# A fused state-space and GELU kernel: decay rows spread by transfers in place of products with ones, and the second weight's pieces queued first

## The chip, the cores and the metric

One Trainium2 chip, one of its cores. The metric is the device time of one launch in microseconds, the median of several runs. One further execution is taken by the hardware profiler; the views below come from it.

## The reference

First a Mamba-2 style scan over 4 batches, 8 heads, 768 positions, head size 32 and state size 16, in chunks of 32, then a feed-forward block over the 3072 tokens.

```python
log_a = np.log(np.clip(a, 1e-06, 1.0))
for c in range(nc):                       # chunks
    cum = np.cumsum(la, axis=-1)
    L = np.exp(cum[:, :, :, None] - cum[:, :, None, :]) * causal
    M = np.einsum('bhin,bhjn->bhij', Cc, Bc) * L
    y_intra = np.einsum('bhij,bhjd->bhid', M, xc)
    y_inter = np.einsum('bhin,bhnd->bhid', Cc, state) * np.exp(cum)[..., None]
    y[:, :, sl] = y_intra + y_inter
    state = decay_full * state + (Bc, xc outer products, decayed to the chunk's end)
x = y.transpose(0, 2, 1, 3).reshape(3072, 256)
h = x @ w_in                              # 256 x 2048
g = h * (1.0 / (1.0 + np.exp(-1.702 * h)))
out = g @ w_out                           # 2048 x 256
```

The two weights are float64 in memory; the kernel turns their bits into float32 on the chip. The other inputs are float32.

## The kernel before, in words

**Tiling.** The 768 positions of a batch are 6 chunks of 128 (NC), and each chunk is two halves of 64 (H), within which the decay matrix L is made. Work goes by *pairs* of chunks, all 8 heads at once: 12 pairs, 3 to a batch. Pairs are numbered over the batches, so pairs 0, 1 and 2 are batch 0 and pairs 3 to 5 batch 1. PG = 2 pairs make a *group* of 512 tokens (TG), and there are 6 groups. Pair 2 (PG) and pair 3 are group 1; pair 2 is the third and last pair of batch 0, and its rows are that batch's last 256 positions.

**Stages of a pair.** `decay(p)` makes L: one VectorE scan over the pair's a, spread over 128 partitions (`ra[p]`), against `idents`, a tile that starts a new product at the diagonal; `ends` multiplies B by L's last column into Be. `clip_rows(b)` and `decay_rows(b)` make `since[b]`, the decay since the start of a half, from the batch's a spread over partitions (`raf[b]`): clip on VectorE, the first elements set apart by GpSimd, a scan on VectorE. `turn(p)` transposes B and C on TensorE, ScalarE copies them from PSUM, and `since_start` multiplies C by `since` on VectorE, reading the transposed C in PSUM. `score` is the product C by B, `gain` the product Be by x into two PSUM banks A, `keep_both` turns A into states, `weigh` multiplies L by the scores, and `finish` has the products of y: step 0 from states (inter), step 1 from L and x (intra).

**The feed-forward block** of group 0 is `hidden(0, f)` for 16 values of f, two matmuls of 512 columns each and a Silu, and `project_all(0, ...)`, again 16 values of f with two matmuls of 512 columns each. Later groups do it by a seven-product scheme (`first`, `product`), with sums of weights prepared by `mix_in` and `mix_w` on VectorE.

**Weights.** w_in and w_out are read in 10 pieces (0 to 5 of w_in, 6 to 9 of w_out, 1 MB each for 4 to 9). `fetch(i)` issues the two transfers of a piece into one of 4 buffers of bits; `rounded`, `fields`, `clamp` and `join` convert it, on VectorE but for `clamp` on ScalarE. `narrow(i)` is `rounded(i)`, `fields(i + 1)`, `join(i)`. A buffer is free when the `join` of the piece before in it has read it.

**The order** is written out by hand. While `hidden(0, f)` and `project_all(0)` run, two tables, `in_hidden[0]` and `in_project[0]`, say what is put behind or ahead of which f:

```python
    at(in_hidden[0], 5, store_a, lambda: fetch(7), lambda: fetch(8),
       lambda: load(PG + 1))
    at(in_hidden[0], 9, lambda: fan_all(PG))
```

Every engine executes its instructions in that order (`in_order`). Nearly all transfers are issued by SyncE (SP), so its queue has the same order, and an issue that waits holds back all behind it. Transfers wait on one of 8 semaphores in turn, so a transfer is issued only after the eighth before it has landed.

**How a is spread.** The decay needs each row of a on 64 or 128 partitions. For pairs 0 and 1 it comes from logarithms and matmuls. `rows_a` loads a into `az`, four copies of 32 rows (one row to a batch and head); `clip(az)` clips it, sets each half's first element apart in `starts` and zeroes it. `store_a` then writes the 32 rows to a scratch tensor in DRAM, and for pair 3 and later `spread(p)` reads it back, the same 2 KB to each of 64 partitions (256 runs of 2 KB for a pair). `spread_rows(b)` does the like for a batch's rows straight from a. For pair 2 it is done by products with ones: `pick_a` (ScalarE) masks the rows by head, `fan_all` issues 8 matmuls with `ones` (`fan`, L412), then those of the last rows of batch 0 (`fan_since`, L501 and L530) with `whose`, then four VectorE scans straight from PSUM (`decay_heads`). `since_fanned` scans the last rows into `since[0]`.

The tile of `raf` has one buffer for all batches (tag "af", bufs=1).

Of the kernel before, what the change touches and what calls it, by code (L numbers as in the profile page):

```python
# [8 lines left out]
FP32 = mybir.dt.float32  # L9
# [26 lines left out]
def kernel(  # L36
# [69 lines left out]
    az = ffn.tile([P, 4 * TG // 2], FP32, tag="mg", name="az", bufs=3)[:, :NC * P].rearrange(  # L106
# [138 lines left out]
    def spread(p, held=False):  # L245

        if p - 2 in ra:
            ra[p] = ra[p - 2]
        else:
            ra[p] = words(f"a{p}").bitcast(FP32)[:, :2 * NH * H].rearrange(  # L250
                "p (k e) -> p k e", k=2)
        if held:
            nc.vector.memset(ra[p][:, 0, :1], 0.0)
        b, c = divmod(2 * p, NC)
        for i, side in enumerate(SIDES):
            nc.sync.dma_start(
                out=ra[p][side],
                in_=scratch[c:c + 2, i, b * NH:(b + 1) * NH].rearrange("c h i -> c (h i)").unsqueeze(
                    0).to_broadcast([H, 2, NH * H]))
# [3 lines left out]
    def spread_rows(b):  # L263
        raf[b] = raw.tile([P, NC, P], FP32, tag="af", name=f"af{b}", bufs=1)
        nc.sync.dma_start(out=raf[b].rearrange("p c s -> p (c s)"),
                          in_=a[b].unsqueeze(1).to_broadcast([NH, N, S]))

    def rows_a(t, queues):

        e = t.shape[1] * P  # L270
        for r in range(R):
            queues[r % len(queues)].dma_start(
                out=t[32 * r:32 * r + 32].rearrange("p c s -> p (c s)"),
                in_=a.rearrange("b h s -> (b h) s")[:, :e])
# [74 lines left out]
    starts, fans, flat = {}, {}, {}  # L349

    def clip(t, name):

        nc.vector.tensor_scalar(out=t, in0=t, scalar1=1e-6, scalar2=1.0,
                                op0=ALU.max, op1=ALU.min)
        starts[name] = const.tile([P, t.shape[1], 2], FP32, name=f"starts{name}")
        first = t.rearrange(by_chunk, s=2)[:, :, :, 0]
        nc.vector.tensor_copy(starts[name], first)
        nc.vector.memset(first, 0.0)

    def pick_a(p):  # L360

        b, c = divmod(2 * p, NC)
        X = ffn.tile([P, 2, DM], FP32, tag="ob", name=f"X{p}")
        X = fans[p] = X.rearrange("p k (q i) -> p k q i", q=Q)
        for q in range(Q):
            nc.scalar.activation(X[:, :, q], az[:, c:c + 2], AF.Copy, scale=pick[:, b, q:q + 1])

# [9 lines left out]
    pick = picker("pick", NB, 1, NH)  # L377
    whose = const.tile([32 * PG, 1 + PG, NH, N], FP32, name="whose")
    nc.gpsimd.memset(whose, 1.0)
    for i, n, head in ((0, 1, PG), (1, 2, PG), (0, 0, 1)):  # L380
        t = whose[32 * i:32 * i + 32, n:n + 1]
        nc.gpsimd.affine_select(out=t, in_=t, pattern=[[-1, 1], [-head, NH], [0, N]],
                                compare_op=ALU.is_equal, fill=0.0, base=-max(n - 1, 0),
                                channel_multiplier=1)
# [23 lines left out]
    def fan(p, r, ab):  # L408

        rows = slice(32 * r, 32 * r + 32)  # L410
        for i, side in enumerate(SIDES):
            nc.tensor.matmul(out=ab[side].rearrange("p (k q i) -> p k q i", k=2, q=Q),  # L412
                             lhsT=ones[rows, side], rhs=fans[p][rows][:, :, :, side],
                             start=True, stop=True, tile_position=(32 * r, H * i),
                             skip_group_check=True)

    def fan_all(p):

        ab = area(f"ab{p}")[:, :, :2 * Q * H]
        for r in range(R):  # L420
            fan(p, r, ab[:, r])
        fan_since()
        for r in range(R):
            decay_heads(p, r, ab[:, r])
        for k in range(2):
            ends(p, k)

# [15 lines left out]

    def decay_heads(p, r, ab):

        if r == 0:
            L = ssd.tile([P, R, 2 * Q * H], FP32, tag="L", name=f"L{p}", bufs=3)
            flat[p] = L
            Ls[p] = L.rearrange("p r (k q i) -> p k r q i", k=2, q=Q)
        nc.vector.tensor_tensor_scan(  # L450
            out=flat[p][:, r], data0=ab,
            data1=idents.rearrange("p h i -> p (h i)")[:, :2 * Q * H],
            initial=0.0, op0=ALU.mult, op1=ALU.add)
# [24 lines left out]
    def clip_rows(b):  # L478
        t = raf[b]
        nc.vector.tensor_scalar(out=t, in0=t, scalar1=1e-6, scalar2=1.0,  # L480
                                op0=ALU.max, op1=ALU.min)
        first = ssd.tile([P, NC, P], FP32, tag="first", name=f"first{b}", bufs=1)
        nc.gpsimd.memset(first, 0.0)
        f, t0 = (v.rearrange(by_chunk, s=2)[:, :, :, 0] for v in (first, t))
        nc.gpsimd.tensor_copy(f, t0)
        nc.gpsimd.memset(t0, 0.0)
        firsts[b] = first

    def decay_rows(b):

        t, first = raf.pop(b), firsts.pop(b)
        since[b] = ssd.tile([P, NC, P], FP32, tag="since", name=f"since{b}")
        nc.vector.tensor_tensor_scan(
            out=since[b].rearrange("p c s -> p (c s)"), data0=t.rearrange("p c s -> p (c s)"),
            data1=first.rearrange("p c s -> p (c s)"),
            initial=0.0, op0=ALU.mult, op1=ALU.add)

    def fan_rows(t, c0, c1, o):

        o = o[:, :(c1 - c0) * P]  # L500
        nc.tensor.matmul(out=o, lhsT=whose[:32, 0].rearrange("p h n -> p (h n)"),  # L501
                         rhs=t[:32, c0:c1].rearrange("p c s -> p (c s)"), start=True,
                         stop=True, tile_position=(0, 0), skip_group_check=True)
        return o

    def since_first():
# [3 lines left out]
        for p in range(PG):  # L510
            at = slice(32 * p, 32 * p + 32)
            nc.tensor.matmul(out=rows[p],
                             lhsT=whose[at, 1 + p].rearrange("p h n -> p (h n)"),
                             rhs=cum[at].rearrange("p k s -> p (k s)"), start=True, stop=True,
                             tile_position=(32 * p, 0), skip_group_check=True)
# [9 lines left out]

    def fan_since():
        o = bank("rows4")
        t = fanned["rows"] = fan_rows(az, CG, NC, o)
        f = fanned["starts"] = o[:, 2 * P:2 * P + 2 * (NC - CG)]
        nc.tensor.matmul(out=f, lhsT=whose[:32, 0].rearrange("p h n -> p (h n)"),  # L530
                         rhs=starts[1][:32, CG:].rearrange("p c s -> p (c s)"), start=True, stop=True,
                         tile_position=(0, 0), skip_group_check=True)

    fanned = {}

    def since_fanned():

        t, f = fanned["rows"], fanned["starts"]
        first = ssd.tile([P, NC, P], FP32, tag="first", name="first0", bufs=1)[:, CG:]
        nc.gpsimd.memset(first, 0.0)  # L540
        nc.vector.tensor_copy(first.rearrange(by_chunk, s=2)[:, :, :, 0],
                              f.rearrange("p (c s) -> p c s", s=2))
        nc.vector.tensor_tensor_scan(
            out=since[0][:, CG:].rearrange("p c s -> p (c s)"), data0=t,
            data1=first.rearrange("p c s -> p (c s)"), initial=0.0, op0=ALU.mult, op1=ALU.add)
# [38 lines left out]
    def area(name):  # L584
        return psa.tile([P, R, 4 * P], FP32, tag="cb", name=name)
# [605 lines left out]
    rows_a(az, (nc.sync,))  # L1191
# [20 lines left out]
    load(PG)  # L1212
# [7 lines left out]
    def store_a():  # L1220
        clip(az, 1)
        for i, side in enumerate(SIDES):
            nc.sync.dma_start(out=scratch[:, i].rearrange("c r i -> r c i"), in_=az[:32, :, side])

    at(in_hidden[0], 5, store_a, lambda: fetch(7), lambda: fetch(8),
       lambda: load(PG + 1))
    at(in_hidden[0], 6, lambda: pick_a(PG))
    at(in_hidden[0], 9, lambda: fan_all(PG))
    at(in_hidden[0], 9, since_fanned)
    for i, k, c in ((2, 1, 1), (3, 2, 2), (4, 4, 4), (5, 6, 8), (6, 9, 12), (7, 12, 15)):  # L1230
        at(in_hidden[0], k, lambda i=i: narrow(i))
        at(in_hidden[0], c, lambda i=i: clamp(i + 1))
    at(in_hidden[0], 9, lambda: spread(PG + 1), lambda: spread_rows(1))
    n, p = 2 * PG, 3 * PG
    pairs = PG, PG + 1
    at(in_project[0], 0, lambda: turn(PG), lambda: rounded(8), lambda: fold_ident(1),
       lambda: fields(9), lambda: join(8))
    at(in_project[0], 1, lambda: clamp(9))
    at(in_project[0], 2, lambda: decay(PG + 1), lambda: clip_rows(1),
       lambda: decay_rows(1), lambda: turn(PG + 1))  # L1240
    at(in_project[0], 5, lambda: narrow(9))
    at(in_project[0], 9, lambda: score(pairs), lambda: gain(pairs), lambda: keep_both(pairs, True),
# [202 lines left out]
```

## Time and profile before

| | us |
|---|---|
| median of 3 runs | 351.66 |
| lowest and highest | 350.62, 352.45 |
| the profiled execution, whole run | 349.68 |
| its span, first to last instruction | 347.8 |
| TensorE (PE) busy | 342.0 (98%) |
| VectorE (DVE) busy | 253.5 (73%) |
| ScalarE (ACT) busy | 153.1 (44%) |
| GpSimd (POOL) busy | 12.9 (4%) |

How to read it: the whole run is the span and some 1.9 us around it. PE is the matmuls, PEld the weight loads, which overlap them. Busy shares are means over the span; the stage with the change lies in its first quarter, from 17.8 us (first hidden unit) to 80 us (last product of group 0's projection). Times of single instructions are us from the span's start. In the chain of waits, each matmul counts twice or nearly so, since a float32 matmul leaves two records.

### The profile page before, as it was taken

The numbers are of one execution on the slowest core, as the hardware profiler recorded it, in microseconds if no ns is written. First come the engines' busy times: TensorE is split into PE (matmuls) and PEld (weight loads), VectorE is DVE, ScalarE is ACT, GpSimd is POOL, SyncE is SP. The second block draws the span as 40 slices with busy tenths as digits, with TensorE's granted clock in tenths as the row PEclk, the third lists the DMA queues.
The fourth block names the chain that finished last, engine by engine and source line by source line (L and its number), as shares of the span: only waits on it lengthen the run. The fifth ranks groups of instructions, "written<-read, shape, count | busy, mean of one in ns | idle before, by whom it ended". The sixth has DMA issues, their size and how long they took to land.

```text
span 347.8 us, 8141 instructions
## 1 busy us (share of the span) xinstructions
PE 342.0 (98%) x3392; PEld 271.9 (78%) x3392; DVE 253.5 (73%) x479; ACT 153.1 (44%) x349; POOL 12.9 (4%) x41
## 2 busy tenths in 40 slices
PE   8899999999999999999999999999999999999996
PEld 6644444557788888888888888888888888899996
DVE  5899999998679998839995649787555654455463
ACT  5698573107354324744332543442444321554320
POOL 8300000000000100000000000000000000000000
PEclk9999999999999999999999999999999999999999
DMA  6699997435526100435613036300000300000301
GB/s 162 142 336 193 283 212 155 81 77 93 105 58 128 33 2 15 63 104 102 101 28 50 2 81 117 64 2 1 2 2 2 61 2 0 0 2 0 62 0 61
DMA packets 89980, 25.92 MB, mean 75 GB/s; under 512 B 73432, under 2 KB 87128, under 8 KB 89944
## 3 DMA queue, kind: packets, MB, share of 16 engines
q1 hardware_dynamic: 89112, 24.88, 33.3%
q10 hardware_dynamic: 832, 0.52, 0.5%
q8 instruction: 26, 0.43, 0.5%
q14 instruction: 10, 0.08, 0.1%
HBM read 22.15 MB, written 3.24 MB: 73 GB/s over the span
## 4 chain that ended last, share of the span: by engine, by line
PE 97%; ACT 1%; DVE 1%; issue 0%; DVEq 0%
PE acc L1050 28%; PE X L945 20%; PE Y L955 14%; PE h L889 10%; PE o L987 8%; PE acc L1057 7%; PE y L833 2%; PE y L821 2%; PE cb L682 2%; PE A L713 1%; PE busy L440 1%; PE ab L554 1%; PE ab L548 0%; DVE steps L735 0%; ACT steps L730 0%; ACT drop L522 0%
## 5 line engine op out<-in xcount | busy, mean ns | idle before, releaser
L950 ACT ACTIVATE ac<-X 128x256 f32<-128x256 f32 x76 | 29.1, 383 | 78.6 <-PE X L945 78.2
L1050 PE MATMUL acc<-mg,mw 128*128 128x256 f32 x192 | 54.5, 379 | 0.0
L922 ACT ACTIVATE gT<-gT 128x512 f32<-128x512 f32 (+1 forms) x76 | 39.3, 520 | 34.1 <-DVE gT L1077 33.4
L1077 DVE TENSOR_TENSOR gT<-Y,ac 128x512 f32<-128x512 f32 x38 | 26.2, 689 | 36.1 <-PE Y L955 30.5
L945 PE MATMUL X<-my,mi 128*128 128x256 f32 x152 | 45.2, 380 | 0.0
L1077 DVE TENSOR_TENSOR gT<-Y,b 128x256 f32<-128x256 f32 x38 | 15.8, 419 | 35.2 <-PE Y L955 35.2
L1050 PEld LDWEIGHTS acc<-mg,mw 128*128 128x128 f32 x192 | 36.5, 190 | 5.0
L1050 PE MATMUL acc<-gT,w_out 128*128 128x256 f32 x128 | 35.5, 379 | 0.0
L889 PE MATMUL h<-yT,w_in 128*128 128x512 f32 (+2 forms) x98 | 35.5, 518 | 0.0
L945 PEld LDWEIGHTS X<-my,mi 128*128 128x128 f32 x152 | 28.0, 190 | 4.1 <-ACT ac L950 0.4
L889 PEld LDWEIGHTS h<-yT,w_in 128*128 128x128 f32 x98 | 17.0, 190 | 16.5 <-issue 14.3
L987 PE MATMUL o<-gT,w_out 128*128 128x512 f32 x64 | 28.6, 597 | 0.0
L913 DVE TENSOR_TENSOR mg<-gT 128x512 f32<-128x512 f32 x40 | 27.2, 681 | 0.0
L1050 PEld LDWEIGHTS acc<-gT,w_out 128*128 128x128 f32 x128 | 24.2, 190 | 3.4 <-ACT yT L860 0.2
L950 ACT ACTIVATE b<-X 128x256 f32<-128x256 f32 x38 | 14.6, 384 | 20.0 <-PE X L945 19.6
L945 PE MATMUL X<-yT,w_in 128*128 128x256 f32 x76 | 23.2, 389 | 0.0
L945 PE MATMUL X<-my,w_in 128*128 128x256 f32 x76 | 22.7, 382 | 0.2 <-issue 0.2
L955 PE MATMUL Y<-yT,w_in 128*128 128x256 f32 x76 | 22.7, 381 | 0.0
L955 PE MATMUL Y<-my,mi 128*128 128x256 f32 x76 | 22.6, 379 | 0.0
L955 PE MATMUL Y<-yT,mi 128*128 128x256 f32 x76 | 22.5, 379 | 0.0
L987 PEld LDWEIGHTS o<-gT,w_out 128*128 128x128 f32 x64 | 11.8, 190 | 13.2 <-issue 12.7
L402 DVE TENSOR_TENSOR_SCAN L<-a,idents 128x1024 f32<-128x1024 f32 x9 | 20.5, 2277 | 0.4 <-DMA a<-scratch 0.4
(156 smaller groups left out, 544.2 us busy)
## 6 DMA issues: line engine op xcount, KB each, us to landing
a<-scratch SPq DMA_DIRECT2D x18, 256.0 KB, 5.3
bits<-in_moe_w_out_dram SPq DMA_DIRECT2D x8, 512.0 KB, 5.4
x<-in_x_dram SPq DMA_DIRECT2D x24, 128.0 KB, 3.0
out_dram<-ob SPq DMA_DIRECT2D x40, 64.0 KB, 1.9
bits<-in_moe_w_in_dram SPq DMA_DIRECT2D x8, 256.0 KB, 4.6
bits<-in_moe_w_in_dram SPq DMA_DIRECT2D x4, 512.0 KB, 9.3
b<-in_B_dram SPq DMA_DIRECT2D x20, 64.0 KB, 3.0
af<-in_a_dram SPq DMA_DIRECT2D x3, 384.0 KB
```

Source lines behind the costliest of these rows:

```text
L402: nc.vector.tensor_tensor_scan(out=L, data0=ra[p].rearrange("p k e -> p (k e)"), data1=idents.rearrange("p h i -> p (h i)"), initial=0.0, ...
L682: nc.tensor.matmul(out=s["cb"][side, r, k].rearrange("p (q i) -> p q i", q=Q), lhsT=BT[rows, k, side], rhs=CT[rows, k, :, side], start=Tru ...
L889: nc.tensor.matmul(out=h[:, cols], lhsT=w_in[:, f, k], rhs=yT[g][:, k, cols], start=(k == 0 and e == 0), stop=(k == NK - 1), skip_group_ch ...
L913: nc.vector.tensor_tensor(out=t[:, 0:2], in0=B[:, :, 1], in1=B[:, 0], op=ALU.subtract)
L922: nc.scalar.activation(o, i, AF.Silu, scale=GELU_SCALE)
L945: nc.tensor.matmul(out=s["X"], lhsT=lhsT, rhs=rhs, start=i == "1", stop=i == "4", skip_group_check=True)
L950: nc.scalar.activation(copy, s["X"], AF.Copy)
L955: nc.tensor.matmul(out=o, lhsT=lhsT, rhs=rhs, start=s.pop("new", False), stop=i != "5", skip_group_check=True)
L987: nc.tensor.matmul(out=o[c], lhsT=w_out[:, c, f], rhs=gT[g, f // 2][:, f % 2], start=(f == 0), stop=(f == NF - 1), skip_group_check=True)
L1050: nc.tensor.matmul(out=acc[g][0][i][:, cols], lhsT=w, rhs=h[:, cols], start=(j == 0 and k == 0 and (i, 0) in begins), stop=(j == NF // 2 - ...
L1057: nc.tensor.matmul(out=o[k] if type(o) is list else o[:, cols], lhsT=h[:, cols], rhs=w, start=(j == 0 and (i, k) in begins), stop=(j == NF ...
L1077: nc.vector.tensor_tensor(out=o, in0=v, in1=w, op=ALU.add)
```

## The change

Pair 2's a and the last 256 positions' rows of batch 0 are spread by transfers like those of the later pairs. `az` has 32 rows only, loaded by one transfer. `clip`, `pick_a`, `fan`, `fan_all`, `decay_heads`, `fan_rows`, `fan_since`, `since_fanned`, the mask `pick` and a third of `whose` go. `spread(PG)` uses a buffer of yT. `spread_rows(0)` reads the last two chunks alone.

The order changes with it. On SyncE, piece 7 of w_out is fetched after f=3, piece 8 after f=5 behind the stores to scratch, then B and C of pair 2 (piece 9 follows when piece 5 is joined), after f=9 the rows of batch 0, the a of pair 2, B and C of pair 3, the a of pair 3, then the x of both; the rows of batch 1 come after f=4 of the projection and wait until the scan of batch 0's rows has freed their buffer. Before, B, C and x of pair 2 went ahead of pieces 7 and 8, and those of pair 3 ahead of piece 9. In the projection `turn(PG)` goes from f=0 to f=3, pair 2's decay is behind it, pair 3's block goes from f=2 to f=5, `narrow(9)` from f=5 to f=6, and `score` and `gain` from f=9 to f=10.

```diff
-    az = ffn.tile([P, 4 * TG // 2], FP32, tag="mg", name="az", bufs=3)[:, :NC * P].rearrange(
+    az = ffn.tile([P, 4 * TG // 2], FP32, tag="mg", name="az", bufs=3)[:32, :NC * P].rearrange(
...
     def spread(p, held=False):
 
-        if p - 2 in ra:
+        if p == PG:
+            ra[p] = ffn.tile([P, NK, TG], FP32, tag="yT", name=f"a{p}").rearrange(
+                "p (k x) s -> p k (x s)", k=2)
+        elif p - 2 in ra and p - 2 > PG:
             ra[p] = ra[p - 2]
...
     def spread_rows(b):
-        raf[b] = raw.tile([P, NC, P], FP32, tag="af", name=f"af{b}", bufs=1)
+        c = 0 if b else CG
+        raf[b] = raw.tile([P, NC, P], FP32, tag="af", name=f"af{b}", bufs=1)[:, c:]
         nc.sync.dma_start(out=raf[b].rearrange("p c s -> p (c s)"),
-                          in_=a[b].unsqueeze(1).to_broadcast([NH, N, S]))
+                          in_=a[b, :, c * P:].unsqueeze(1).to_broadcast([NH, N, S - c * P]))
...
-    rows_a(az, (nc.sync,))
+    nc.sync.dma_start(out=az.rearrange("p c s -> p (c s)"), in_=a.rearrange("b h s -> (b h) s"))
...
-    load(PG)
...
     def store_a():
-        clip(az, 1)
+        nc.vector.tensor_scalar(out=az, in0=az, scalar1=1e-6, scalar2=1.0, op0=ALU.max, op1=ALU.min)
+        nc.vector.memset(az.rearrange(by_chunk, s=2)[:, :, :, 0], 0.0)
         for i, side in enumerate(SIDES):
-            nc.sync.dma_start(out=scratch[:, i].rearrange("c r i -> r c i"), in_=az[:32, :, side])
-
-    at(in_hidden[0], 5, store_a, lambda: fetch(7), lambda: fetch(8),
-       lambda: load(PG + 1))
-    at(in_hidden[0], 6, lambda: pick_a(PG))
-    at(in_hidden[0], 9, lambda: fan_all(PG))
-    at(in_hidden[0], 9, since_fanned)
+            nc.sync.dma_start(out=scratch[:, i].rearrange("c r i -> r c i"), in_=az[:, :, side])
+
+    at(in_hidden[0], 3, lambda: fetch(7))
+    at(in_hidden[0], 5, store_a, lambda: fetch(8), lambda: load(PG, "bc"))
...
-    at(in_hidden[0], 9, lambda: spread(PG + 1), lambda: spread_rows(1))
+    at(in_hidden[0], 9, lambda: spread_rows(0), lambda: spread(PG), lambda: load(PG + 1, "bc"),
+       lambda: spread(PG + 1), lambda: load(PG, "x"), lambda: load(PG + 1, "x"))
+    at(in_project[0], 4, lambda: spread_rows(1))
     n, p = 2 * PG, 3 * PG
     pairs = PG, PG + 1
-    at(in_project[0], 0, lambda: turn(PG), lambda: rounded(8), lambda: fold_ident(1),
-       lambda: fields(9), lambda: join(8))
-    at(in_project[0], 1, lambda: clamp(9))
-    at(in_project[0], 2, lambda: decay(PG + 1), lambda: clip_rows(1),
-       lambda: decay_rows(1), lambda: turn(PG + 1))
-    at(in_project[0], 5, lambda: narrow(9))
-    at(in_project[0], 9, lambda: score(pairs), lambda: gain(pairs), lambda: keep_both(pairs, True),
-       lambda: weigh(PG), lambda: weigh(PG + 1))
+    at(in_project[0], 0, lambda: rounded(8), lambda: fields(9), lambda: join(8))
+    at(in_project[0], 2, lambda: clamp(9))
+    at(in_project[0], 3, lambda: clip_rows(0), lambda: decay_rows(0), lambda: turn(PG),
+       lambda: fold_ident(1), lambda: decay(PG))
+    at(in_project[0], 5, lambda: decay(PG + 1), lambda: clip_rows(1),
+       lambda: decay_rows(1), lambda: turn(PG + 1))
+    at(in_project[0], 6, lambda: narrow(9))
+    at(in_project[0], 10, lambda: score(pairs), lambda: gain(pairs), lambda: keep_both(pairs, True),
+       lambda: weigh(PG), lambda: weigh(PG + 1))
```

More of the change, by code (lines that the diff above doesn't have):

```diff
@@ L263, in spread_rows @@
     def spread_rows(b):
-        raf[b] = raw.tile([P, NC, P], FP32, tag="af", name=f"af{b}", bufs=1)
+        c = 0 if b else CG
+        raf[b] = raw.tile([P, NC, P], FP32, tag="af", name=f"af{b}", bufs=1)[:, c:]
         nc.sync.dma_start(out=raf[b].rearrange("p c s -> p (c s)"),
-                          in_=a[b].unsqueeze(1).to_broadcast([NH, N, S]))
[L268 to L274, printed above, removed]
+                          in_=a[b, :, c * P:].unsqueeze(1).to_broadcast([NH, N, S - c * P]))
     for r in range(R):
@@ L347 @@
         data1=cum.rearrange("p k s -> p (k s)"), initial=0.0, op0=ALU.mult, op1=ALU.add)
[L349 to L366, printed above, removed]
+    flat = {}
     same = ssd.tile([P, NH, D], FP32, tag="BT", name="same")
@@ L376 @@
         fill=0.0, base=N - 1, channel_multiplier=-1)
-    pick = picker("pick", NB, 1, NH)
-    whose = const.tile([32 * PG, 1 + PG, NH, N], FP32, name="whose")
+    whose = const.tile([32 * PG, PG, NH, N], FP32, name="whose")
     nc.gpsimd.memset(whose, 1.0)
[L380 to L383, printed above, removed]
+    for n in range(PG):
+        t = whose[32 * n:32 * n + 32, n:n + 1]
+        nc.gpsimd.affine_select(out=t, in_=t, pattern=[[-1, 1], [-PG, NH], [0, N]],
+                                compare_op=ALU.is_equal, fill=0.0, base=-n,
                                 channel_multiplier=1)
@@ L406, in decay @@
             ends(p, k)
[L408 to L426, printed above, removed]
     def pads(n, t):
@@ L442, in keep_busy @@
                              start=True, stop=True, skip_group_check=True)
[L444 to L453, printed above, removed]
     def ends(p, k):
@@ L481, in clip_rows @@
                                 op0=ALU.max, op1=ALU.min)
-        first = ssd.tile([P, NC, P], FP32, tag="first", name=f"first{b}", bufs=1)
+        first = ssd.tile([P, NC, P], FP32, tag="first", name=f"first{b}", bufs=1)[:, NC - t.shape[1]:]
         nc.gpsimd.memset(first, 0.0)
@@ L491, in decay_rows @@
         t, first = raf.pop(b), firsts.pop(b)
-        since[b] = ssd.tile([P, NC, P], FP32, tag="since", name=f"since{b}")
+        if b not in since:
+            since[b] = ssd.tile([P, NC, P], FP32, tag="since", name=f"since{b}")
         nc.vector.tensor_tensor_scan(
-            out=since[b].rearrange("p c s -> p (c s)"), data0=t.rearrange("p c s -> p (c s)"),
+            out=since[b][:, NC - t.shape[1]:].rearrange("p c s -> p (c s)"), data0=t.rearrange("p c s -> p (c s)"),
             data1=first.rearrange("p c s -> p (c s)"),
             initial=0.0, op0=ALU.mult, op1=ALU.add)
[L498 to L504, printed above, removed]
     def since_first():
@@ L512, in since_first @@
             nc.tensor.matmul(out=rows[p],
-                             lhsT=whose[at, 1 + p].rearrange("p h n -> p (h n)"),
+                             lhsT=whose[at, p].rearrange("p h n -> p (h n)"),
                              rhs=cum[at].rearrange("p k s -> p (k s)"), start=True, stop=True,
@@ L524, in drops @@
                 1).to_broadcast([P, Q * D, 2 * CG - 1]))
[L526 to L545, printed above, removed]
     def mask(t, new):
```

## The prediction

> **What bounds the kernel now.** I read the chain of work that ended last first, narrowed to the stage that the change touches, then the timelines of VectorE and SyncE there, then the windows for the DMA rates. The chain (start us, us, what):
>
> ```profile
> 17.79 17.52 PE h L889 x40
> 35.31 0.62 PE ab L412 x16
> 35.93 0.62 PE rows L501 x2
> 36.55 0.12 PE rows L530 x2
> 36.67 10.50 PE h L889 x24
> 47.17 0.44 PE tp L597 x4
> ...
> 63.50 1.14 PE cb L682 x63
> 64.63 0.72 PE A L713 x47
> ...
> 80.35 3.51 PE h L889 x24
> 83.86 0.86 PE A L713 x49
> ```
>
> From 17.8 us to the end TensorE is the chain with hardly a gap: the next matmul is always ready. So each microsecond of matmuls removed is gained whole, until another engine is late. The products with ones (L412, L501, L530) are 0.62 + 0.62 + 0.12 = 1.36 us of that chain.
>
> VectorE comes second and has little room (start us, us, line, operation, tiles):
>
> ```profile
> 57.26 2.28 DVE L402 TENSOR_TENSOR_SCAN L<-a,idents 128x1024 f32<-128x1024 f32 x1
> 59.57 0.49 DVE L461 TENSOR_TENSOR Be<-b,L 128x128 f32<-128x128 f32 x2
> 59.98 0.55 DVE L480 TENSOR_SCALAR af<-af 128x768 f32<-128x768 f32 x1
> 61.09 1.76 DVE L493 TENSOR_TENSOR_SCAN since<-af,first 128x768 f32<-128x768 f32 x1 [0.55 <-POOL af L486]
> 62.98 0.42 DVE L667 TENSOR_TENSOR CsT<-tp,since 128x256 f32<-128x256 f32 x1
> 63.32 1.22 DVE L208 SCALAR_TENSOR_TENSOR m<-bits,m 128x1024 f32<-128x1024 uint32 x1
> ...
> 82.12 0.49 DVE L461 TENSOR_TENSOR Be<-b,L 128x128 f32<-128x128 f32 x2
> ```
>
> From L480's start to CsT's end is 3.42 us; from there to the last Be of pair 5, at 82.61, there are 19.21 us of VectorE work without a gap worth naming. TensorE takes that Be in the second half of the A products, at 83.86 + 0.43 = 84.29. VectorE's slack is thus 1.7 us, over the whole stage.
>
> Third, DMA. The windows from 37 to 75 us (window, length, PE, PEld, DVE, ACT and POOL busy, clock, DMA share, GB/s):
>
> ```profile
> 37.00:42.00 5.00, 5.00 (x13) 2.23 (x12) 4.93 (x10) 1.88 (x4) 0.46 (x1) 1.00 1.01 335
> 43.00:45.60 2.60, 2.60 (x7) 1.14 (x6) 2.57 (x4) 2.40 (x3) 0.00 (x0) 1.00 1.00 99
> 50.80:59.00 8.20, 8.20 (x23) 3.86 (x22) 7.58 (x9) 3.75 (x7) 0.00 (x0) 1.00 0.91 187
> 71.00:75.00 4.00, 4.00 (x64) 2.12 (x63) 3.90 (x12) 0.00 (x0) 0.00 (x0) 1.00 0.49 136
> ```
>
> The DMA engines are full until 59 us, and at four rates: w_out alone 335 GB/s, B and C rows 99, two spreads of a with the rows (af) between them 187, one spread alone 136. Nobody waits for it yet: of the waits only one of 0.2 us (VectorE for w_out's last piece) is a DMA's. So the question is what the new order makes late.
>
> **The change, part by part.** All times are of the profiled execution (span 347.8, run 349.68 us); 1.9 us lie around the span, and the run is 2.0 under the median 351.66, so I add the difference found to the median.
>
> *TensorE.* The products leave: -1.36 us. Nothing is added; score and gain move from before f=9 of the projection to before f=10, which moves no time by itself. The clock is 1.00 in all windows, before and after the gap that closes.
>
> *VectorE's work.* Out: the copy of starts and its step (32.71 to 32.94, of which the memset stays: -0.19), the four scans of 256 (2.43) for one of 1024 (2.28), the copy of first (0.20). In: the clip of 256 columns (0.29). The scan of the batch's last rows stays as it was (0.69 against 0.7). Sum -0.25, with the waits for tp (0.38) and w_out (0.21) gone and one of 0.55 for GpSimd added, as L493 shows. That is even or slightly better: nothing lost here.
>
> *ScalarE, GpSimd.* The two activations for X (0.91) and GpSimd's pick mask (about 1.4 at 4.6 us) go. Both are worth nothing: ScalarE idles 0.9 and 1.1 us around that place for TensorE; GpSimd's mask of C starts at 7.69 because the transposed C ends at 7.59, and all that goes is in front of it. Without that cover it would be at most 0.1.
>
> *DMA.* Out: three of four loads of az (96 KB each, under 1 us together). In: the spread of a for pair 2 (512 KB, 256 runs of 2 KB) and 128 KB of rows. Moved: w_out's pieces 7, 8 and 9 ahead; the x of both pairs to the end; the rows af of batch 1 behind x, and behind the VectorE scan that frees the one af buffer.
>
> **Where the new order ends.** With the loads of pair 2 gone from before it, piece 7 goes at about 26.5 us, when join(3) frees its buffer, and has landed by 33. Then SyncE waits for the clip of az (VectorE, 32.8) and issues the two stores to scratch and piece 8 behind them; before, piece 7 showed its rate 1.4 us after issue at 35.42, so piece 8 flows from about 35.5. From there the queue is full, and I add it up in order:
> - piece 8, 1.05 MB at 335 GB/s: 3.1
> - B, C of pair 2: 4096 runs of 64 bytes; 43.0 to 45.6 moved 3802 packets, so 2.8, but 4.2 where the queue was not backed up (30.1 to 34.4): 3.5
> - piece 9: 3.1
> - 128 KB of rows: 0.4 at w_out's rate, 1.7 at the rate of its larger kin; nearest is the spread's 136 GB/s, also a broadcast: 0.9
> - spread of pair 2: 3.1 (in the 8.2 us with another) to 4.3 (5.4 from issue to landing less the 1.1 of issue); alone it took 3.9 for 0.53 MB: 3.6
> - B, C of pair 3: 3.0; its spread: 3.6
> - x of both: 4096 packets at 1580 in 1.3 us: 3.4
> - rows of batch 1, 384 KB: 1.2 at w_out's rate to 2.9 at 136 GB/s; between two spreads 8.2 - 2 x 3.1 = 2.0: 2.0
>
> Together 26.2, to 61.7, and 0.6 for the last landing (piece 8's packets ended at 43.0 and it landed at 43.6): **62.3 us**, with 60 and 67 as the ends.
>
> [...]
>
> VectorE arrives there as follows: az clipped, piece 5 starts at 32.75, three pieces of 4.72 (rows 32.94, 37.66, 41.34 and 46.06) to 46.9, piece 8 with piece 9's fields 4.75 to 51.65 (piece 9 has landed at 45.8), rows and CsT of pair 2 1.8, idents 0.68, two decays of 2.72 to 59.5. The spreads are there in time (50 and 57 us), pair 3's C at 53 before TensorE turns it at about 54.7. At 59.5 it wants the rows of batch 1 and gets them at 62.3: **a wait of 2.8 us**. Then CsT is done at 62.3 + 3.4 = 65.7, and pair 5's last Be 19.2 later at 84.9; the products can take it at 85.0 against 84.29: **+0.7 us**. So the 1.36 is taken back and a little more. In short the difference is the landing of those rows less 61.6, and never under -1.36.
>
> Behind VectorE's wait queue w_out's last piece, the states and the weighing; each would come 0.7 to 1.5 before TensorE asks. Behind SyncE's wait for the af buffer (free at 53.1, while x is still being issued, so hidden) queue the a, z, b and x of pairs 4 and 5. Today the last of them, pair 5's a (issued at 70.13, 5.4 to landing, 75.5), lands 15.6 us after pair 4's a (issued at 50.33, 9.6 to landing, 59.95); so 61.7 + 3.6 + 15.6 = 80.9, wanted by pair 5's decay at 82.2.
>
> **Rivals.** *All lands in time.* If the rows land by 60.2 (the spreads at 3.1, runs of 64 bytes at 2.8), only TensorE's saving stays: -1.36, median 350.3. For it: the share of 0.49 in 71 to 75 us shows room for other transfers beside a spread. Against: at 51 to 59 us the share was 0.91 and nothing overlapped. *The queue is longer* (the other side): same place, VectorE before L480's successor, but the transfers take their long ends: spreads 4.3, rows 1.7 and 2.9, B and C 4.2. That is +1.4 +0.8 +0.9 +1.9 = 5 us, landing at 67, +5.4. It decides as slower from a landing of 63.4 (+1.76 us), only 1.1 over my sum; at the middle of it, 65.2, median 355.3. For it: VectorE has no cover at all there, every late transfer counts fully, and pair 3's C, 1.7 us ahead of TensorE, would be late as well. Against: the whole sum must be wrong in one direction. *The change doesn't do it*: the compiled order has the products gone, the transfers in and piece 8 queued ahead of both pairs' loads, so no chance is kept for that.
>
> **How the numbers follow.** One measurement of this kernel tells about 0.5% (1.76 us) from no change. Forecast, a partial stall of -0.9 to +1.76: 0.35. In time, at the floor: 0.24, and as the floor is -0.4%, spread of the medians (350.62 to 352.45 in three runs) puts 0.07 of it past -0.5%. Longer queue: 0.40. Anything else: 0.01, counted as faster. That gives faster 0.08, same 0.52, slower 0.40. The predicted time is the forecast's, 351.66 + 0.7 = 352.4. The range goes down to the floor and a little spread, 350.0, and up into the longer queue to 356.0 (+4.3, a landing at 65.9), leaving out about 1 in 10 on each side.
>
> **What would show it.** Right: no L412, L501, L530 products; TensorE's hidden units done at about 45.7; VectorE idle 2 to 3 us before the clip of 768 columns, released by a DMA of af; TensorE idle before the A or the score products near 83 us; DMA share near 1 until 62. Wrong: that clip starts at 59.5 without a wait (in time), VectorE waits for a spread, or TensorE waits in the turn of pair 3 (the queue longer, earlier). A loss that sits before 17 us or after 100 us would make the whole working wrong.

## The result, and the profile after

The changed kernel takes **354.25 us** (median of 6 runs, 353.19 to 356.67), the kernel before 350.67 beside it (6 runs, 349.61 to 352.45): a ratio of 1.0108, 95% interval 1.0083 to 1.0134, slower by 3.6 us. The profiled execution of after took 354.37 us, its span is 352.4; before's was 349.68 and 347.8, so the two profiles lie 4.6 us apart, a microsecond more than the medians: before's profile is near the lowest of its times.

The chain of work that ended last, after (start us, us, what; line numbers are after's: L426 is the clip of the rows, L440 their scan, L585 CsT, L631 A):

```profile
58.19 6.57 DMA af<-in_a_dram
64.78 0.57 DVE af L426
65.47 0.21 POOL first L431
65.88 1.77 DVE since L440
67.77 0.44 DVE CsT L585
68.25 0.78 PE A L631 x47
69.03 7.04 PE o L905 x12
...
84.00 3.51 PE h L807 x24
87.52 0.77 PE A L631 x50
```

Where TensorE ran through before, the chain now comes from the transfer of the rows of batch 1 and goes through VectorE before TensorE takes it up with A. VectorE's timeline says how long it stood still:

```profile
60.42 0.49 DVE L407 TENSOR_TENSOR Be<-b,L 128x128 f32<-128x128 f32 x2
64.78 0.56 DVE L426 TENSOR_SCALAR af<-af 128x768 f32<-128x768 f32 x1 [3.87 <-DMA af<-in_a_dram]
65.88 1.76 DVE L440 TENSOR_TENSOR_SCAN since<-af,first 128x768 f32<-128x768 f32 x1 [0.54 <-POOL af L432]
67.77 0.42 DVE L585 TENSOR_TENSOR CsT<-tp,since 128x256 f32<-128x256 f32 x1
...
86.96 0.50 DVE L407 TENSOR_TENSOR Be<-b,L 128x128 f32<-128x128 f32 x2
```

The clip starts at 64.78 where it started at 59.98 before, and pair 5's last Be ends at 87.46 where it ended at 82.61: 22.7 and 22.6 us after the clip. TensorE's timeline:

```profile
65.34 0.30 PE L631 MATMUL A<-x,Be 64*32 64x64 f32 x2
68.25 0.78 PE L631 MATMUL A<-x,Be 64*32 64x64 f32 x54 [2.62 <-DVE CsT L585]
68.96 7.11 PE L905 MATMUL o<-gT,w_out 128*128 128x512 f32 x12
...
83.84 3.68 PE L807 MATMUL h<-yT,w_in 128*128 128x128 f32 x24
87.44 0.84 PE L631 MATMUL A<-x,Be 64*32 64x64 f32 x56
...
152.86 0.95 PE L751 MATMUL y<-L,x 64*32 64x64 f32 x71
154.97 0.79 PE L751 MATMUL y<-L,x 64*32 64x64 f32 x57 [1.16 <-issue]
```

It stops 2.62 us inside A: A's second bank still holds the transposed C that CsT reads. The 12 products after it take 7.11 us. And far behind, in the middle of one run of short products, it stops 1.16 us, which the profile puts down to issue: TensorE waited for nothing that it lists.

The windows (window, length, busy time of PE, PEld, DVE, ACT, POOL, granted clock, DMA share, GB/s):

```profile
33.00:36.00 3.00, 3.00 (x8) 1.33 (x7) 2.95 (x6) 1.81 (x4) 0.00 (x0) 1.00 0.30 73
36.00:42.00 6.00, 6.00 (x15) 2.67 (x14) 5.95 (x7) 4.29 (x7) 0.00 (x0) 1.00 1.04 218
42.00:43.00 1.00, 1.00 (x3) 0.38 (x2) 0.98 (x1) 0.97 (x2) 0.00 (x0) 1.00 0.13 22
43.00:59.00 16.00, 16.00 (x45) 7.47 (x44) 15.20 (x19) 9.21 (x14) 1.03 (x3) 1.00 1.05 179
60.00:62.00 2.00, 2.00 (x6) 0.80 (x6) 0.88 (x3) 0.00 (x0) 0.00 (x0) 1.00 0.55 157
...
70.00:71.00 1.00, 1.00 (x2) 0.34 (x1) 0.97 (x2) 0.74 (x4) 0.00 (x0) 0.50 1.14 180
71.00:72.00 1.00, 1.00 (x2) 0.34 (x1) 0.92 (x2) 0.00 (x0) 0.00 (x0) 0.50 0.63 126
```

Two things to see: the DMA engines run at 0.30 from 33 to 36 us and at 0.13 from 42 to 43, are full on average from 43 to 59 (1.05), and fall to 0.55 from 60 to 62, while the rows of batch 1 are on their way; and after TensorE's stop its clock is halved (0.50) for 3.4 us.

By stage, the profiled executions differ so (TensorE's timeline, first before, then after):

```profile
17.78 17.53 PE L889 MATMUL h<-yT,w_in 128*128 128x512 f32 x40
...
47.44 3.60 PE L987 MATMUL o<-gT,w_out 128*128 128x512 f32 x8
...
80.19 3.68 PE L889 MATMUL h<-yT,w_in 128*128 128x128 f32 x24
```

```profile
18.39 27.83 PE L807 MATMUL h<-yT,w_in 128*128 128x512 f32 x64
46.06 5.31 PE L905 MATMUL o<-gT,w_out 128*128 128x512 f32 x12
```

The first h starts at 18.39 instead of 17.78 us (+0.61; little of the change lies ahead of it, and it varied from 17.78 in before to 18.85 in products_new_queue over the fourteen profiles of this study, so this part is most likely chance). From there to the first o it is 27.67 instead of 29.66 us (-1.99: the products are gone, and 0.44 of transposes, `tp`, have moved behind that point). From the first o to the first h of group 1, 37.77 instead of 32.74 (+5.03: 2.62 the stop in A, 1.7 half of the 3.4 us at half clock, 0.44 the transposes). From there to the end, 268.57 instead of 267.62 (+0.95). The sum is +4.60.

### The profile page after: what moved, and what is told of

The parts are those of the page before. It is cut to its first block, busy times and chain, and to the rows that moved or that the text cites. A ratio compares the mean times of both kernels' runs of the same rounds, so it can differ in the third digit from the quotient of the medians.

```text
span 352.4 us, 8090 instructions
## 1 busy us (share of the span) xinstructions
PE 342.2 (97%) x3372; PEld 272.2 (77%) x3372; DVE 253.4 (72%) x475; ACT 152.4 (43%) x347; POOL 12.0 (3%) x37
## 4 chain that ended last, share of the span: by engine, by line
PE 80%; DVE 9%; DMA 5%; issue 2%; SPq 2%; POOL 0%; DVEq 0%; POOLq 0%
PE acc L968 28%; PE X L863 19%; PE Y L873 14%; PE acc L975 7%; DMA bits<-in_moe_w_in_dram 4%; PE o L905 4%; PE y L751 2%; PE h L807 2%; DMA af<-in_a_dram 2%; DVE p L222 2%; PE cb L600 2%; PE y L739 1%; DVE m L208 1%; DVE p L192 1%; DVE m L195 1%
## 5 line engine op out<-in xcount | busy, mean ns | idle before, releaser
L905 PE MATMUL o<-gT,w_out 128*128 128x512 f32 x64 | 30.5, 626 | 0.0
L868 ACT ACTIVATE b<-X 128x256 f32<-128x256 f32 x38 | 14.6, 383 | 20.0 <-PE X L863 19.5
L379 DVE TENSOR_TENSOR_SCAN L<-a,idents 128x1024 f32<-128x1024 f32 x10 | 22.8, 2281 | 0.2 <-DMA a<-scratch 0.2
L873 PE MATMUL Y<-yT,w_in 128*128 128x256 f32 x76 | 22.7, 381 | 0.0
L873 PE MATMUL Y<-my,mi 128*128 128x256 f32 x76 | 22.6, 379 | 0.0
L863 PE MATMUL X<-my,w_in 128*128 128x256 f32 x76 | 22.6, 381 | 0.0
```

The source lines that it names most:

```text
L379: nc.vector.tensor_tensor_scan(out=L, data0=ra[p].rearrange("p k e -> p (k e)"), data1=idents.rearrange("p h i -> p (h i)"), initial=0.0, ...
L863: nc.tensor.matmul(out=s["X"], lhsT=lhsT, rhs=rhs, start=i == "1", stop=i == "4", skip_group_check=True)
L868: nc.scalar.activation(copy, s["X"], AF.Copy)
L873: nc.tensor.matmul(out=o, lhsT=lhsT, rhs=rhs, start=s.pop("new", False), stop=i != "5", skip_group_check=True)
L905: nc.tensor.matmul(out=o[c], lhsT=w_out[:, c, f], rhs=gT[g, f // 2][:, f % 2], start=(f == 0), stop=(f == NF - 1), skip_group_check=True)
```

## The experiments

Each was timed against the kernel before on the same chip; each profile is of one execution.

**Is it the one buffer?** The rows of batch 0 get a tile of their own.

```diff
-        raf[b] = raw.tile([P, NC, P], FP32, tag="af", name=f"af{b}", bufs=1)[:, c:]
+        if b:
+            raf[b] = raw.tile([P, NC, P], FP32, tag="af", name=f"af{b}", bufs=1)
+        else:
+            raf[b] = ffn.tile([P, 2, DM], FP32, tag="ob", name="af0")[:, 0]...
```

> The changed kernel, with the rows of batch 0 in a tile of their own, so that the rows of batch 1 need not wait until the scan has freed the one af buffer; their place in the queue, behind both pairs' x, is kept. Theory (the transfers ahead of them make these rows late, not the buffer): they are issued at about 58 us and land at about 64.5 as in the changed kernel, VectorE still waits 3 to 4 us for them, time +2.5 to +3.8 us against before. Rival (SyncE's wait for the buffer makes them late): the wait falls under 1.5 us and the time to before's or below.

Measured 353.94, ratio 1.0096 (1.0065 to 1.0126), as slow as the change. In VectorE's timeline the wait for the rows is still there, so the buffer is not its cause:

```profile
66.03 0.56 DVE L430 TENSOR_SCALAR af<-af 128x768 f32<-128x768 f32 x1 [4.39 <-DMA af<-in_a_dram]
```

**Is it the rows' place in the queue?** As own_buffer, and the rows of batch 1 are queued ahead of both x.

```diff
-       lambda: spread(PG + 1), lambda: load(PG, "x"), lambda: load(PG + 1, "x"))
-    at(in_project[0], 4, lambda: spread_rows(1))
+       lambda: spread(PG + 1), lambda: spread_rows(1), lambda: load(PG, "x"), lambda: load(PG + 1, "x"))
```

> As own_buffer, and the rows of batch 1 are queued ahead of both pairs' x. Theory: they land some 3.5 us earlier, at about 61, VectorE's wait falls from 3.9 to under 0.5 us, no drop of the clock, x lands at about 64.5, just ahead of the A products at 65; only the 1.36 us of removed products remain: -1.4 to -0.5 us against before. Rival (the whole queue is too long, whatever its order): the A products wait 2 us or more for x, and the time stays 1.5 to 3.5 us over before.

A miss: 353.88, ratio 1.0076 (1.0048 to 1.0104). The wait for the rows is gone from VectorE's timeline, and in its place it waits for pair 5's a, which lies further down the same queue; TensorE then waits 1.27 us for that pair's Be:

```profile
83.78 2.29 DVE L383 TENSOR_TENSOR_SCAN L<-a,idents 128x1024 f32<-128x1024 f32 x1 [1.75 <-DMA a<-scratch]
```

What was taken from one transfer another paid: moving these rows forward did not help by itself.

**Which part of the change?** First, the transfers' order without the transfers (the products kept, the queue as in after), then the transfers without the new order.

```diff
 # products_new_queue, against before
-    load(PG)
...
-    at(in_hidden[0], 5, store_a, lambda: fetch(7), lambda: fetch(8),
-       lambda: load(PG + 1))
+    at(in_hidden[0], 3, lambda: fetch(7))
+    at(in_hidden[0], 5, store_a, lambda: fetch(8), lambda: load(PG, "bc"))
...
-    at(in_hidden[0], 9, lambda: spread(PG + 1), lambda: spread_rows(1))
+    at(in_hidden[0], 9, lambda: load(PG + 1, "bc"), lambda: spread(PG + 1), lambda: load(PG, "x"),
+       lambda: load(PG + 1, "x"), lambda: spread_rows(1))
 # old_queue, against after
+    load(PG)
...
-    at(in_hidden[0], 3, lambda: fetch(7))
-    at(in_hidden[0], 5, store_a, lambda: fetch(8), lambda: load(PG, "bc"))
+    at(in_hidden[0], 5, store_a, lambda: fetch(7), lambda: fetch(8), lambda: load(PG + 1))
...
-    at(in_hidden[0], 9, lambda: spread_rows(0), lambda: spread(PG), lambda: load(PG + 1, "bc"),
-       lambda: spread(PG + 1), lambda: load(PG, "x"), lambda: load(PG + 1, "x"))
+    at(in_hidden[0], 9, lambda: spread_rows(0), lambda: spread(PG), lambda: spread(PG + 1))
```

> The kernel before (products with ones) with the new order of the queue alone: piece 7 at f=3, piece 8 at f=5, B and C before the pieces' end, both x behind the spread of pair 3, the rows of batch 1 behind x. Theory: without the 512 KB spread and the 128 KB of rows, all lands in time; time within -0.5 to +0.7 us of before. Rival (the new order alone makes x or the rows late): +1.5 to +3.5 us.

> The transfers with the queue order of before: pair 2's x, B, C early, w_out's pieces 7 and 8 at step 5 of hidden, pair 3's loads ahead of piece 9, then rows of batch 0, both spreads, rows of batch 1. Theory (the queue's sum decides, whatever its order): the rows of batch 1 land near 64.6 as in the changed kernel; piece 9 lands near 53.5, as before, where VectorE now wants it at 49, a wait of 4 to 5 us that falls within its wait for the rows; 354 to 356. Rival (the new order is what cost the time): within 0.5 us of before, 351.4.

The order alone is level with before: 351.36, ratio 1.0007 (0.9990 to 1.0024). Its profile, of the slowest of its ten executions (353.22), does show VectorE waiting 1.33 us for the rows, so the new order makes them late by a little on its own. The transfers in the old order took 355.43, 1.0141 (1.0114 to 1.0168), by the median more than the whole change, though the two intervals overlap. VectorE waits 3.52 us there for w_out's last piece, before it comes to the rows, and TensorE 3.95 us for CsT. So the transfers cost the time; that the new order gives some of it back is likely, not shown. VectorE's timeline in old_queue:

```profile
54.46 0.69 DVE L192 TENSOR_SCALAR p<-bits 128x1024 uint32<-128x1024 uint32 x1 [3.52 <-DMA bits<-in_moe_w_out_dram]
```

**Which transfer, and why is it slow?** Pair 2's a filled by GpSimd instead; then that and the last rows of batch 0, so that neither products nor transfers are left; then the same bytes from distinct addresses.

```diff
 # no_spread2
+        if p == PG:
+            nc.gpsimd.memset(ra[p], 0.9)
+            return
 # no_transfers, besides
+        if b == 0:
+            nc.gpsimd.memset(raf[b], 0.9)
+            return
 # distinct2, shortened: for pair 2, the source in place of scratch
+                     x[i].rearrange("h s d -> (h s d)")[:2 * H * NH * H].rearrange("(c r e) -> r c e", c=2, r=H)
```

> The changed kernel without the transfer of pair 2's a: GpSimd fills the tile with 0.9 instead, so pair 2's decay is left out of the result. 512 KB leave the queue. Theory (queue length): the rows of batch 1 land 3.3 to 4 us earlier, VectorE's wait is under 0.8 us, time -1.4 to 0 us against before. [...] Rival (these rows are late for a reason of their own, such as their issue): wait 3 us or more, +2.5 or more.

> The changed kernel with the third pair's a and the last rows of batch 0 filled by GpSimd memsets of 0.9 (their true decays are left out), so neither the products nor the two transfers that took their place remain. Theory (the products were worth 1.36 us on TensorE and the transfers' place in the DMA queue took it all back): rows of batch 1 land by 61.5, VectorE waits under 0.6 us for them, TensorE under 0.3 us for CsT, and the time is 0.7 to 1.4 us under before, some 350.2. Rival (taking the products away is worth nothing, another engine bounds the stretch): 351.4, with a wait of TensorE of a microsecond or more elsewhere before 100 us.

> The changed kernel with the third pair's a filled by the same 512 KB, in the same runs of 2 KB and at the same place in the queue, but from 64 different addresses of x for each side instead of one row read 64 times (pair 2's decay is left out). Theory A (64 reads of one address are what makes a spread slow, 136 GB/s against the 335 GB/s of the pieces): the transfer takes 1.6 instead of 3.6 us, the rows of batch 1 land about 2 us sooner (62.6), the wait of VectorE falls from 3.9 to about 1.9 and that of TensorE from 2.6 to about 0.7, the time is about 2 us under the changed kernel's, some 352. Theory B (the runs' length or the SBUF side sets the rate): no change, 354.

Without pair 2's spread: 351.36, ratio 1.0002 (0.9983 to 1.0021); VectorE's wait for the rows is 1.26 us, a little over what was expected, and the loss is gone. So, in this order of the queue, this one transfer of 512 KB makes the loss. With distinct addresses the time stays, 354.53, 1.0102 (1.0077 to 1.0126), with a wait of 3.83 us: that one row is read 64 times is not what makes the spread slow. no_transfers is a miss: nothing waits for a DMA, and yet it is not faster than before, 351.01 against 350.52, 1.0018 (1.0000 to 1.0036). With after's order of the rest, the removed products alone bring no time that can be measured. Its profile has two losses of its own: 1.7 us of half clock at 18.2 us, and a stop of 0.76 us inside y, of which more below.

**What is the halved clock worth?** 8 products of ones in TensorE's wait.

```diff
+        for i in range(8 if pairs[0] == PG else 0):
+            nc.tensor.matmul(out=A[0][:, 4 * H:], lhsT=ones,
+                             rhs=ones[:, :H].unsqueeze(1).to_broadcast([P, 4, H]),
+                             start=True, stop=True, skip_group_check=True)
```

> The changed kernel with 8 products of ones with ones (128x256, 0.28 us each, 2.2 us together) between the third and fourth pair's C B products and their A products, in the half of A's PSUM bank that A does not use: they lie in TensorE's wait of 2.62 us for CsT and delay nothing if the rows of batch 1 land as in the profile of after. Theory (the idle gap halves the clock, a second cost of 1.7 us): the granted clock stays at 1.00 from 69 to 73 us, the 12 partial products of o after A take about 5.3 us instead of 7.04, and the time is about 1.2 us under the changed kernel's 354.25 (four of its six executions had the mean clock of 0.995), some 353. Rival (the halving comes for another reason and the gap has no part in it): a stretch of 3.4 us at 0.50 still follows A, and the time stays at 354.3 or rises.

TensorE's timeline and one of its windows:

```profile
65.83 3.72 PE L623 MATMUL A<-ones 128*128 128x256 f32 x16
69.48 0.79 PE L635 MATMUL A<-x,Be 64*32 64x64 f32 x56
70.20 5.42 PE L909 MATMUL o<-gT,w_out 128*128 128x512 f32 x12
```

```profile
71.00:72.00 1.00, 1.00 (x3) 0.38 (x2) 0.89 (x3) 0.99 (x5) 0.00 (x0) 1.00 0.85 157
```

The clock stays at 1.00 and the 12 products take 5.42 instead of 7.11 us: the idle time did halve it. Time 353.43, ratio 1.0072 (1.0053 to 1.0092), near the 353 of the theory, but the clock can hardly be its reason. The products of ones lasted 3.72 us, not 2.2, since each left two records (x16), and A began 1.2 us later than in after; still pair 5's Be ends at 87.25, by VectorE's own chain, and TensorE takes its half of A at 87.44, against 87.46 and 87.75 in after. What the clock costs TensorE in after is 1.7 us by the two rows; how much reaches that point is 0.3 at most in these profiles, because VectorE is no earlier. For the medians it is open: of after's six executions the four with a mean clock of 0.995 took 354.14 to 356.67 us, the two with 1.00 took 353.19 and 353.95.

**The gap inside y.** In all fourteen profiles, TensorE's idle time of 0.25 us or more put down to issue within y<-L,x stood ahead of its matmul number 349 (in twelve), 854 (in two) or 1743 (in eight) of the program, counted from 0. Number 1743 is the 72nd of a run of 128 in after and the 52nd in before, whose program is 20 matmuls longer up to there. In before that run has no stop:

```profile
149.50 1.57 PE L833 MATMUL y<-L,x 64*32 64x64 f32 x128
```

10 tiny products, 20 matmuls by the records (y<-ones x20), were added, early in code_shift (in TensorE's wait for the first state; part of y is lost there and in early_loads_shift).

```diff
                 intra(n, p)
+            pads(10, begun_y["free"])
             for t in range(NK):
```

> The changed kernel with 20 products of ones (32x32, 22 ns each, 0.44 us together) in TensorE's wait of 0.5 to 0.7 us for the first state, ahead of y<-CsT,S near 16 us: TensorE's program is as long again as before from there on, nothing else differs. In ten profiles TensorE's idle time put down to issue within y<-L,x came only ahead of its products number 349, 854 and 1743, whatever these products were; after the change 1743 is the 72nd of its run of 128 short products, before it was the 52nd. Theory (a place in TensorE's program, not the data, makes this gap, and the 20 removed products moved it): no gap near 155 us, the time from the first h of the second group to the end is 267.7 instead of 268.6 us, the median about 0.8 us under the changed kernel's, some 353.5, with the wait of 2.6 us for CsT and the halved clock as they were. Rival (the gap belongs to the data or the moment): a gap of 0.8 to 1.2 us near 155 us still, 354.3.

```profile
20.94 5.40 PE L810 MATMUL h<-yT,w_in 128*128 128x512 f32 x8 [1.86 <-ACT p L204]
...
153.12 1.57 PE L753 MATMUL y<-L,x 64*32 64x64 f32 x128
```

The run of 128 is whole, in 1.57 us; the time is 353.42, ratio 1.0071 (1.0044 to 1.0099), 0.8 under the change, though the two intervals overlap. It was not as clean as expected: TensorE also lost 1.86 us to ScalarE and 1.7 to a halved clock from 21.6 to 25.0 us, and had no wait at CsT; behind A its clock stayed at 1.00, and it then waited 1.00 us for VectorE's L. Yet its A for pair 5's Be comes at 87.50, against 87.75, since VectorE's Be ends at 87.32. Over all profiles the gap at number 1743 is there (0.76 to 1.16 us) in the eight kernels with after's count up to that place, and in none of the six that have 16 or 20 more. In these six, number 1743 lies in the same run, as its 52nd or 56th product, so the number alone does not make the stop.

The traces show what goes with it: the transfers of a DMA queue of another kind, "instruction", 16 KB each, 26 in every run. One ran from 152.32 to 153.61 us in after, as its DMA queues from 152 to 154 us show (queue, kind: packets, MB, share of 16 engines):

```profile
q8 instruction: 1, 0.02, 4.0%
```

All 22 stops, at 349, 854 and 1743, ended 1.2 to 1.5 us after the latest of these transfers. In the eight kernels with the stop at 1743 it had begun 0.5 to 0.7 us ahead of the run of 128, in the six without it 3.6 to 3.9 us ahead. That TensorE waits there for its next instructions is the author's estimate from these times; no run changes the transfers alone.

**Can the queue be shortened?** As own_buffer, and pair 2's B and C into the idle time from 33 us, pair 3's behind w_out's piece 8, the rows of batch 1 between both x.

```diff
-    at(in_hidden[0], 3, lambda: fetch(7))
-    at(in_hidden[0], 5, store_a, lambda: fetch(8), lambda: load(PG, "bc"))
+    at(in_hidden[0], 3, lambda: fetch(7), lambda: load(PG, "bc"))
+    at(in_hidden[0], 5, store_a, lambda: fetch(8), lambda: load(PG + 1, "bc"))
...
-    at(in_hidden[0], 9, lambda: spread_rows(0), lambda: spread(PG), lambda: load(PG + 1, "bc"),
-       lambda: spread(PG + 1), lambda: load(PG, "x"), lambda: load(PG + 1, "x"))
-    at(in_project[0], 4, lambda: spread_rows(1))
+    at(in_hidden[0], 9, lambda: spread_rows(0), lambda: spread(PG), lambda: spread(PG + 1),
+       lambda: load(PG, "x"), lambda: spread_rows(1), lambda: load(PG + 1, "x"))
 # early_loads_pads, besides, ahead of the A products
+            pads(10, A[0][:, 4 * H:])
```

> The changed kernel with pair 2's B and C queued at step 3 of hidden, where the DMA engines run nearly idle from 33 to 36 us in the profile of after, pair 3's B and C behind w_out's piece 8, the rows of batch 1 between both x, and the rows of batch 0 in a tile of their own so that nothing waits for a buffer. Theory (the sum of the queue from 35 us is what made the rows late; 3.5 us of it fit in idle time before): rows of batch 1 land before 60, VectorE waits under 0.5 us for them, TensorE not at all for CsT, no halved clock after A; the changed kernel's 354.25 less 2.6 less the clock's 1.2: some 350.5, within 0.4 per cent of before, the removed products being nearly paid back by the gap at product 1743. Rival (pieces of w_out or pair 5's a are now late, as in rows_ahead): 352 to 354, with a wait of over a microsecond for bits or a.

> early_loads with the 20 short products of code_shift. Theory: as early_loads, less the gap of 0.8 us at product 1743: 349.7, some 0.2 to 0.4 per cent under before, the only version of these to be under it. Rival (the products' 1.36 us were never there to be had in the total): 350.5 to 351, level with before and with early_loads.

> early_loads with the 20 short products of ones (0.44 us) ahead of the third and fourth pair's A products instead, so that nothing before 65 us changes; in early_loads TensorE waits 0.77 us for VectorE's L at 72.5 us, so the products take no time of their own. Theory (place in TensorE's program): no gap of issue near 151 us, no wait added elsewhere, some 350.1 against early_loads' 350.8 and before's 350.9, a ratio to before near 0.998. Rival (the gap in the profile does not add to the time, or the products delay A and so L): 350.8 or more.

early_loads takes 350.82 against 350.92 for before, ratio 1.0000 (0.9979 to 1.0020): the whole loss is gone with all transfers in place. It differs from after in three ways: the earlier B and C, the place of batch 1's rows, and a tile of their own for batch 0's. The tile alone (own_buffer) and the tile with the rows further ahead (rows_ahead) gained nothing clear of their intervals, so the earlier B and C are the likely reason, which no run shows alone. In its VectorE timeline nothing waits for rows, and the clip is still 1.4 us later than before (VectorE's timeline, then TensorE's):

```profile
61.00 0.49 DVE L411 TENSOR_TENSOR Be<-b,L 128x128 f32<-128x128 f32 x2
61.41 0.55 DVE L430 TENSOR_SCALAR af<-af 128x768 f32<-128x768 f32 x1
...
83.58 0.49 DVE L411 TENSOR_TENSOR Be<-b,L 128x128 f32<-128x128 f32 x2
```

```profile
72.51 1.04 PE L743 MATMUL y<-CsT,S 32*64 32x64 f32 x56 [0.77 <-DVE L L615]
...
83.95 0.84 PE L635 MATMUL A<-x,Be 64*32 64x64 f32 x56
```

TensorE, ahead by the products, now waits for VectorE's L and reaches A at 83.95, where it was at 83.79 before; counted from the first h, which is 0.52 later here, that is 0.36 earlier. With the 20 matmuls added to it, early (351.10, 1.0011, 0.9989 to 1.0033) or ahead of A (351.13, 1.0005, 0.9984 to 1.0026), the gap at number 1743 is gone from both profiles and the median did not fall; both expectations missed. The profiled execution of the last was the fastest of its 12 runs (349.87), so its profile cannot say where the median execution loses what the gap would have cost. No version beat both kernels.

## Why the prediction was right and wrong

The time lies in the range, in its upper part, and it came as the rival "The queue is longer" had it, behind the wait that it named and about its middle (355.3 forecast, 354.25 measured). The forecast's own size, +0.7, was too small. Part of its closeness in time is luck: it was added to 351.66, the median of three runs, and before took 350.67 beside after. As a difference, +3.6 was measured against +0.7, and +3.6 is also the middle of the rival.

- **The place held.** VectorE waits before the clip of 768 columns, released by the DMA of af; the products are gone; nothing waited for the buffer or for w_out; pair 5's a landed at 81.25 (80.9 predicted) with no wait.
- **The path behind the wait was another.** The prediction let TensorE stand near 83 us, for pair 5's Be. It stood at 65.6 instead, for 2.62 us, inside the A of pairs 2 and 3, for CsT; the prediction had CsT late at 65.7 and named nobody waiting for it. TensorE came to pair 5's Be without a wait, 0.3 us after it was ready (87.46 and 87.75). The two paths cost nearly the same here, so the time does not tell them apart.
- **The rule "landing less 61.6" came close,** by that coincidence. With 64.78 it gives +3.2; TensorE reached pair 5's products of A at 87.75 instead of 84.10, +3.65. (The prediction's 84.29 is half of the row's time; the first of these products starts at 84.10, so the slack was 1.5 us and not 1.7.) The stretch from clip to last Be was predicted at 22.6 us and lay between 22.6 and 22.8 in after and in ten of the twelve experiments; in no_transfers it was 23.1, and in rows_ahead the wait for a lies inside it.
- **The step that failed is the landing, 62.3, by 2.5 us.** Most of it is the last term of the sum: the rows of batch 1 were put at 2.0 us and took 3.5, from the landing of x at 61.3 to 64.8, more than the rival's long end of 2.9. Their packets ran from 59.6 to 63.7, and the DMA engines were at 0.55 from 60 to 62, where the prediction had them near 1 until 62; why these rows go so slowly is open. The head of the queue was 0.9 late. "From there the queue is full" did not hold: the DMA engines ran at 0.30 until 36 us, SyncE issued piece 8 only at 34.67, behind the stores of a, and it landed at 40.1, where the sum with its 0.6 for a landing has 39.2. Piece 9 landed at 46.7 instead of 45.8; the engines' fall to 0.13 from 42 to 43, when SyncE's issues of C and of piece 9 took 3.39 and 2.18 us with all else queued behind them, fell within what the sum gave to B and C. From piece 9 to x it took 14.6 us and the sum has 14.5, both spreads among them: these rates were right, and of the rival's long ends only that of these rows was reached.
- **The rate of a spread** was read off the row of 71 to 75 us, 136 GB/s, and off its neighbours, and the stretch with both spreads took what the sum gave it (14.6 us against 14.5). Why a spread goes no faster is not shown; distinct2 (354.53, a wait of 3.83 us for the rows) says that the 64-fold reading of one row is not the reason.
- **VectorE's arrival** was put at 59.5 and was 60.9, most of it from a later start of this execution (az was clipped by 33.63, not 32.75).
- **The floor of -1.36 was not reached by any median.** TensorE was shorter from the first h to the first o by the products, as predicted. But VectorE's slack before the last Be was 1.5 us in the profile of before, and where the rows were there in time and w_out's last piece held VectorE by 1.2 us at most (no_transfers and the three early_loads kernels), its clip started at 60.83 to 62.09 against 59.98, and TensorE took that Be at 84.00 to 85.20 against 84.10. Of this, 0.2 to 0.9 us is a later first h (18.01 to 18.63 against 17.78, the earliest of all fourteen). Counted from the first h, TensorE took that Be 0.94 us earlier in early_loads_pads, 0.33 earlier in early_loads, level in no_transfers with its 1.7 us of half clock, and 0.87 later in early_loads_shift. "All lands in time" happened in these four, level with before (1.0000 to 1.0018) and not 1.36 us under it; what takes the saving from the medians is shown only in part.
- **The clock at 1.00 "in all windows" fell,** with 1.7 us on TensorE's rows, of which VectorE's chain hides all but 0.3 in the profiles. In after a gap of 2.62 us, which ended at 68.25, was enough: the clock was 0.50 from 69.4 to 72.8 us, and in fill_idle, without that gap, it stayed at 1.00.
- **A loss behind 100 us,** which the prediction said would make its working wrong, is there in part: +0.95, of it 1.16 the gap inside y. That the number of matmuls ahead decides on it is shown, and code_shift and fill_idle, both without it, are 0.8 under the change; between early_loads and the two kernels made from it, where it should count as much (0.2%), intervals of 0.4% do not show it. That it is the loading of TensorE's program is the author's estimate from the times of 22 stops; no run changes the loading.

## What to carry to other kernels

Here the DMA queue was full (a share of 1.05 from 43 to 59 us in after) nearly up to the moment VectorE wanted its last transfer: what was added landed on that one (a wait of 3.87 us), and moving it forward handed the delay to the next (1.75 us in rows_ahead). What helped, most likely, was to issue other transfers in a stretch in which the queue had room (0.30 from 33 to 36 us in after; early_loads, ratio 1.0000). Add up the queue with its idle stretches and with the issues that hold it, not from the moment the first issue could go. Before counting an engine's saved work as time, ask when the second engine's chain through the same stage would end without it.

## What the runs showed of the hardware

An idle 2.6 to 4.0 us on TensorE was followed by 3.4 us at half clock in after, own_buffer, distinct2 and old_queue, and with products in that time (fill_idle) it was not. In no_spread2 and no_transfers the same halving came at 18.2 us, after the short products and waits of at most 0.8 us, and in code_shift at 21.6 us, after a wait of 1.86; own_buffer, with a wait of 0.97 us among the short products, kept 1.00 there. Runs of short products stopped for 0.3 to 1.2 us, and all 22 such stops ended 1.2 to 1.5 us after a 16 KB transfer of the instruction queue. An edit far ahead added or removed one: with 20 matmuls more at 15.4 us (code_shift), the stop of 1.16 us that after has at 154.97 is gone. That these stops are waits for instructions is the author's estimate from their times; no run shows it.
